# A new DMA model and offline priorities in a kernel's list scheduler, with re-laid DMA transfers: one adaLN transformer block on one Trainium2 core

## The chip, the cores and the metric

One NeuronCore of a Trainium2 chip. The metric is the device time of one launch in microseconds; lower is better. Ratios are the mean time of one kernel's fast runs over the mean of the other's fast runs of the same rounds, so they are not quite the ratios of the medians that are quoted. Profiles are of one execution each and are a microsecond or two shorter than the times, because they run from the first to the last instruction.

## The reference, cut to what matters

```python
mod = (silu(c) @ w_mod)                      # c: 1 x 640, w_mod: 640 x 3840 -> six vectors of 640
sa, ca, ga, sb, cb, gb = ...
h = layernorm(x) * (1 + ca) + sa             # x: 2048 x 640, bf16
qkv = h @ wqkv                               # 640 -> 3*640, 32 heads of 20
scores = q @ k.T * 20**-0.5                  # causal, window of 256 rows back
o = softmax(scores) @ v
x = x + ga * (o @ wo)
h = layernorm(x) * (1 + cb) + sb
x = x + gb * ((sigmoid(h @ w_gate) * (h @ w_up)) @ w_down)    # 640 -> 1536 -> 640
```

## The kernel before

All work is stated as operations with the tiles they read and write. A list scheduler inside the kernel's Python, run when the program is built, picks an order for each engine: it keeps a model of when each engine is free and how long each operation takes, and takes the ready operation with the lowest priority number. On the chip every engine then runs its list strictly in order. TensorE's list mixes small-tile attention matmuls with projections and MLP as filler. Nearly all DMAs are issued from SyncE's list.

A head has 20 columns, and four heads share one tile of 128 partitions, each at a multiple of 32. Projected Q and K come out of TensorE with other rows together, so they are written to a scratch in DRAM and read back in the arrangement for attention:

```python
def proj_qk(cc, mts, halves, prio):                  # chunk cc of 512 rows of x
    for which, (w, Rw) in enumerate(((wq, R_wq), (wk, R_wk))):
        ...                                          # scratch of this chunk: dram [640, 512]
        for mt in mts:
            ...                                      # 128 columns of Q or K for 512 rows: matmuls, eviction to s
            dma(d[mt * 128:(mt + 1) * 128, :], s.ap[:])
        for hh in halves:
            ...
            for j in range(4):                       # 20 partitions each, rows of 1 KB
                dma(t.ap[32*j:32*j + 20, :, :],
                    d.rearrange("(g r) c -> r g c", r=80)[j*20:(j+1)*20, 4*hh:4*hh + 4, :])
```

```python
if o.isdma:                                          # in the scheduler: one pipe of 330 GB/s
    s0 = max(st + dur + 0.3, bw)
    move = o.nbytes / 330e3
    bw = s0 + move
    o.end = s0 + move + o.fix
...
p_stg = sbpool("stg", 3, [128, 512])                 # staging buffers between projection and scratch
```

The first chunk's Q and K are projected "directly" instead: 640 small-tile matmuls that put each head at its partitions, no scratch. LayerNorm outputs of the later chunks are transposed by DMA. (In the listing of proj_qk the lambdas and the reads= and writes= lists are left out.)

The softmax here doesn't subtract the row's maximum and nothing guards it: scores larger than these inputs give would overflow.

## Time and profile before

| | before |
|---|---|
| time, median | 361.6 us (361.2 to 367.8 in 4 runs; the 367.8 counts as slow and is left out of the ratio) |
| profiled span | 358.6 us, granted clock 0.995 (another run, of 360.3 us) |
| TensorE busy | 339.7 us (95%) |
| TensorE idle | 18.9 us |
| DMA, main queue | 41% of 16 engines |

The lines behind this are shown in the prediction below. How they are read: the matmuls are pipelined and their ends are modelled in the profile, so 95% busy is not 95% of TensorE's peak; what TensorE waits for is in the list of waits; the DMA share of a window is the mean over the core's 16 DMA engines.

### The profile page before, as it was taken

The page shows a single profiled execution, that of the slowest core. Times are in us where ns is not written, and L with a number is a line of the kernel's source. Part 1 is how long each engine was busy: PE and PEld are TensorE (multiplying, and loading weights), DVE is VectorE, ACT ScalarE, POOL GpSimd, SP SyncE. Part 2 cuts the span into 40 slices and gives each one's busy share as a digit, 9 for nine tenths or more (in the row PEclk, how much of TensorE's full clock was granted, in tenths as well). Part 3 has the DMA queues.
Part 4 walks back from the last instruction along what each step waited for, and adds up shares of the span by engine and source line. Part 5 has one row for each costly group of instructions (what it writes and reads, how often), then busy time and mean ns, then how long its engine had stood idle before and what let it go on. Part 6 is the DMA issues. An engine that isn't in the chain of part 4 may idle for free.

```text
span 358.6 us, 10125 instructions
## 1 busy us (share of the span) xinstructions
PE 339.7 (95%) x4014; PEld 198.3 (55%) x4038; DVE 233.9 (65%) x504; ACT 223.6 (62%) x231; POOL 182.4 (51%) x304
## 2 busy tenths in 40 slices
PE   7989989989699999999999999999999999999996
PEld 3657556445235564445666534544664454788884
DVE  4569987994678977649787464776677755433342
ACT  1577876768648888887888788678678312022130
POOL 4227855985468975666676565566656201000000
PEclk9999999999989999999999999999999999999999
DMA  6988489696962652431281123003323010310101
GB/s 204 354 295 274 106 185 385 159 194 126 265 208 66 166 80 64 122 118 53 62 140 38 57 74 92 5 20 65 87 89 85 25 42 1 74 38 0 38 1 39
DMA packets 52672, 40.32 MB, mean 112 GB/s; under 512 B 22544, under 2 KB 49424, under 8 KB 52624
## 3 DMA queue, kind: packets, MB, share of 16 engines
q1 hardware_dynamic: 52624, 39.67, 40.7%
q8 instruction: 32, 0.52, 0.6%
q14 instruction: 16, 0.13, 0.1%
HBM read 25.89 MB, written 9.18 MB: 98 GB/s over the span
## 4 chain that ended last, share of the span: by engine, by line
PE 71%; DMA 9%; DVE 7%; SPq 4%; ACT 3%; issue 3%; POOL 1%; DVEq 0%; POOLq 0%
PE M L521 57%; PE S L522 7%; PE O L522 6%; SPq L438 4%; ACT E L802 3%; DMA oT<-doc 2%; DMA dq<-stg 2%; DMA x<-in_A_x_dram 2%; DVE x L602 2%; DMA hT<-x 1%; DMA big<-in_w_mod_dram 1%; PE M L522 1%; PE S L510 1%; DVE T L870 1%; DVE h2T L613 1%
## 5 line engine op out<-in xcount | busy, mean ns | idle before, releaser
L802 ACT ACTIVATE E<-S 128x2048 bf16<-128x2048 f32 (+1 forms) x104 | 171.3, 1647 | 43.2 <-PE S L522 40.4
L818 POOL TENSOR_SCALAR_AFFINE_SELECT E<-E 128x512 bf16<-128x512 bf16 x128 | 82.9, 657 | 84.7 <-ACT E L802 81.5
L521 PE MATMUL M<-h2T,wgu 128*128 128x256 bf16 (+1 forms) x708 | 110.8, 307 | 1.3 <-issue 0.8
L521 PEld LDWEIGHTS M<-h2T,wgu 128*128 128x128 bf16 x720 | 67.1, 98 | 35.5 <-issue 5.7
L820 POOL TENSOR_SCALAR_AFFINE_SELECT E<-E 128x512 bf16<-128x512 bf16 x112 | 73.6, 664 | 0.0
L928 ACT ACTIVATE sig<-M 128x256 f32<-128x256 f32 (+1 forms) x72 | 31.9, 454 | 56.7 <-PE M L521 56.6
L930 DVE SCALAR_TENSOR_TENSOR big<-sig,M 128x256 bf16<-128x256 f32 (+1 forms) x72 | 36.5, 507 | 44.8 <-PE M L521 36.2
L521 PE MATMUL M<-wd,big 128*128 128x320 bf16 x384 | 56.4, 299 | 0.0
L521 PEld LDWEIGHTS M<-wd,big 128*128 128x128 bf16 x384 | 36.5, 98 | 16.5 <-issue 1.9
L522 PE MATMUL S<-QT,KT 20*128 20x256 bf16 (+2 forms) x832 | 38.6, 259 | 3.0 <-ACT E L802 1.9
L522 PE MATMUL O<-E,V 128*32 128x256 bf16 (+2 forms) x832 | 32.4, 263 | 0.7 <-POOL E L818 0.7
L522 PEld LDWEIGHTS S<-QT,KT 20*128 20x128 bf16 x832 | 12.6, 92 | 34.6 <-ACT E L802 20.0
L940 DVE TENSOR_TENSOR x<-M,x 128x320 bf16<-128x320 f32 x32 | 15.6, 488 | 21.4 <-PE M L521 21.2
L870 DVE STREAM_TRANSPOSE T<-O 128x512 f32<-128x512 f32 x32 | 22.7, 711 | 9.6 <-PE O L522 9.0
L591 DVE BATCH_NORM_STATS2 st<-x 128x6 f32<-128x320 bf16 x64 | 27.1, 472 | 1.9 <-DMA x<-in_A_x_dram 1.7
L521 PE MATMUL M<-wo,oT 128*128 128x320 bf16 x160 | 26.1, 300 | 1.2 <-DMA oT<-doc 1.2
L521 PE MATMUL M<-wv,hT 128*128 128x320 bf16 x160 | 25.6, 300 | 1.0 <-DVE hT L651 1.0
L522 PEld LDWEIGHTS O<-E,V 128*32 128x32 bf16 x832 | 15.4, 95 | 15.9 <-issue 7.8
L521 PE MATMUL M<-hT,wk 128*128 128x512 bf16 x70 | 19.2, 398 | 4.1 <-DMA dq<-stg 3.8
L879 DVE STREAM_TRANSPOSE On<-Tn 128x512 bf16<-128x512 bf16 x32 | 22.5, 704 | 0.4
L667 DVE CAST stg<-M 128x512 bf16<-128x512 f32 x19 | 13.1, 690 | 14.3 <-PE M L521 14.2
L602 DVE TENSOR_SCALAR x<-x,st 128x640 bf16<-128x640 bf16 x32 | 19.9, 649 | 2.4 <-POOL st L599 2.3
(59 smaller groups left out, 280.3 us busy)
## 6 DMA issues: line engine op xcount, KB each, us to landing
x<-in_A_x_dram SPq DMA_DIRECT2D x32, 160.0 KB
big<-in_w_mod_dram SPq DMA_DIRECT2D x15, 320.0 KB
doc<-On SPq DMA_DIRECT2D x64, 40.0 KB
out_dram<-x SPq DMA_DIRECT2D x16, 160.0 KB
wgu<-in_B_w_gate_dram SPq DMA_DIRECT2D x5, 384.0 KB
wgu<-in_B_w_up_dram SPq DMA_DIRECT2D x5, 384.0 KB
wd<-in_B_w_down_dram SPq DMA_DIRECT2D x6, 320.0 KB
dq<-stg SPq DMA_DIRECT2D x15, 128.0 KB
```

What stands on the lines that cost most here:

```text
L521: return e.matmul(o, l, r, start=st, stop=sp, skip_group_check=True)
L522: return e.matmul(o, l, r, start=st, stop=sp, tile_position=tp, skip_group_check=True)
L591: ins = e.bn_stats(v(bi * 12 + j * 6, 6), src[bi].ap[:, j * 320:(j + 1) * 320])
L602: A("dve", lambda e, g, bi=bi: e.tensor_scalar(dst[bi].ap[:], src[bi].ap[:], v(48 + 2 * bi, 1), v(60 + bi, 1), op0=ALU.subtract, op1=ALU.m ...
L802: A("act", lambda e, eng, E=E, Sp=Sp, ncol=ncol: e.activation(E.ap[:, :, 0:ncol], Sp.ap[:, :, 0:ncol], ACT.Exp, scale=SM_SCALE), c_act(4 * ...
L818: return e.affine_select(ap, ap, pattern=[[0, 4], [1, 128]], compare_op=ALU.is_ge, fill=0.0, base=0, channel_multiplier=-1)
L820: return e.affine_select(ap, ap, pattern=[[0, 4], [-1, 128]], compare_op=ALU.is_ge, fill=0.0, base=-1, channel_multiplier=1)
L870: A("dve", lambda e, g: e.transpose(T1.ap[:], O.ap[:]), c_dve(512), reads=[O.r()], writes=[T1.r()], prio=4, tag="tr1")
L879: A("dve", lambda e, g: e.transpose(On.ap[:, half * 512:half * 512 + 512], Tn.ap[:]), c_dve(512), reads=[Tn.r()], writes=[On.r(half)], pri ...
L928: A("act", lambda e, g, pg=pg, sg=sg: e.activation(sg.ap[:, 0:W], pg.ap[:, 0:W], ACT.Tanh, scale=0.5), c_act(W), reads=[pg.r()], writes=[s ...
L930: A("dve", lambda e, g, pu=pu, sg=sg, ft=ft: e.scalar_tensor_tensor(out=hv(ft), in0=sg.ap[:, 0:W], scalar=1.0, in1=pu.ap[:, 0:W], op0=ALU. ...
L940: A("dve", lambda e, g, ps=ps, bi=bi, half=half: e.tensor_tensor(x1[bi].ap[:, half * 320:half * 320 + 320], ps.ap[:, 0:320], x1[bi].ap[:, ...
```

## The change

Intent: make the scheduler's picture of DMA truer (issue, descriptor rate, time for each descriptor, write receipt), choose the priorities offline so that the order stands up to random DMA delays, take work off the DMA queue, and read the Q/K scratch in rows of 4 KB. The core of the diff:

```diff
+                acc = max(st + 0.1, dge)
+                free[e] = max(st + dur, acc + 0.3)
+                dge = acc + 0.0018 * o.nd                        # nd: number of descriptors
+                bw = max(acc + 1.15, bw) + o.nd / 16e3 * (9 + o.nbytes / o.nd / 27.2)
+                o.end = bw + (1.2 if o.wr else 1.85)
...
+        o.prio = prio + PRIO.get(o.grp, 0.0)
+PRIO = {"x0": -9.5, "x1": -20.25, "wm0": 78.5, ... }             # 68 entries, cut
...
-    p_stg = sbpool("stg", 3, [128, 512])
+    p_stg = sbpool("stg", 6, [128, 512])
...                                     # c: one row of 1280 bytes and 5 tiny matmuls, not 640 runs of 2 bytes
...                                     # ln1: chunks 1 and 2 transposed on TensorE, evicted with scale and shift
...                                     # one scratch for Q and one for K, [92, 8, 512], used by all chunks
-                    dma(d[mt * 128:(mt + 1) * 128, :], s.ap[:])
+                dma(bass.AP(d.tensor, d.offset + mt * 4096, [[512, 8], [NDT * 4096, 16], [1, cw]]), s.ap[:, 0:cw])
...
-                for j in range(4):     # 4 DMAs of 20 partitions
+                if cw == 512:          # 1 DMA of 128 partitions, 12 rows in 32 not needed
+                    dma(t.ap[:], bass.AP(d.tensor, d.offset + 2048 * hh,
+                                         [[DH * 4096, 4], [4096, 32], [1, 2048]]), ..., nd=128)
...
-            proj_qk_direct(1, 13.6)    # second half of the first chunk
+            proj_qk(0, 12.7, 256, 256)
...                                     # attention pieces of two head groups packed into one tile of 2048
...                                     # attention output: 16 writes of 256 KB instead of 64 of 40 KB
```

(In the code cuts here and below the lambdas and the reads= and writes= lists are left out as well.)

## The prediction

> **What bounds the kernel now.** I read the page's first table, then the busy digits, then the groups by line with the shapes kept apart, then the table of ten-microsecond windows, the waits of TensorE alone, the chain of waits, and last the timeline of the stretches that stood out. Page and windows first:
>
> ```profile
> PE 339.7 (95%) x4014; PEld 198.3 (55%) x4038; DVE 233.9 (65%) x504; ACT 223.6 (62%) x231; POOL 182.4 (51%) x304
> PE   7989989989699999999999999999999999999996
> ...
> 0.00:10.00 10.00, 7.40 (x53) 3.58 (x54) 3.61 (x10) 1.49 (x2) 4.30 (x33) 1.00 0.69 219
> 20.00:30.00 10.00, 8.83 (x204) 6.27 (x206) 7.51 (x19) 6.70 (x9) 3.10 (x6) 1.00 0.81 277
> 90.00:100.00 10.00, 6.58 (x52) 3.03 (x54) 5.30 (x14) 5.33 (x5) 5.22 (x8) 0.99 0.96 279
> 300.00:310.00 10.00, 9.95 (x66) 6.29 (x65) 4.29 (x10) 1.20 (x2) 0.00 (x0) 1.00 0.31 51
> ```
>
> TensorE is busy for 339.7 of 358.6 us; the next engine stands at 65%. So the kernel is bound by TensorE, and idle TensorE time is only 18.9 us: about 2.6 in the first window, 3.4 in the window from 90 us, some 3 after the last matmul, the rest in crumbs. An upper limit follows at once: better waiting alone can give back perhaps 10 us. But busy is not full. I summed columns from the groups (count x columns / 2.4 GHz, divided by four where four small tiles run at once, which is an assumption of the sum): about 300 us for the whole program, 4 of them warm-up. By windows the sum fills some 0.75 of the time from 10 to 60 us, 0.58 from 90 to 100, about 0.84 from 100 to 280, and about 1.0 from 280 on. The timeline shows why it differs so:
>
> ```profile
> 222.54 0.29 PE L522 MATMUL S<-QT,KT 20*128 20x128 bf16 x8
> 222.77 0.51 PE L522 MATMUL O<-E,V 128*32 128x256 bf16 x16
> 223.21 1.25 PE L521 MATMUL M<-h2T,wgu 128*128 128x512 bf16 x5
> ...
> 339.79 9.44 PE L521 MATMUL M<-h2T,wgu 128*128 128x256 bf16 x85
> ```
>
> The score group holds TensorE for 0.23 us (to the next start) where its columns need 0.11; the attention-times-V group holds it 0.44 where they need 0.21. Against that, 85 matmuls of the last MLP take 111 ns each where columns need 107. So each small-tile group costs 0.1 to 0.2 us beyond its columns, at its change of form; such groups interleaved with MLP and projections are what makes 0.84 of 1.0. The waits of TensorE are short:
>
> ```profile
> PE M L521 <- DMA dq<-stg: 3.8, 2, 3.2
> PE S L522 <- ACT E L802: 1.9, 7, 0.5
> PE M L521 <- DMA oT<-doc: 1.2, 2, 0.8
> PE M L521 <- DVE hT L651: 1.0, 1, 1.0
> PE S L522 <- DMA KT<-dk: 0.9, 1, 0.9
> ```
>
> The largest is a projection that can't start because the three staging buffers are still being written to the scratch (3.2 us in one piece). From 300.3 to 355.8 us the chain of waits is one piece of TensorE work, the last MLP chunk, and the change doesn't touch it.
>
> **What the Trainium skill says.** "TensorE: Matmul & The Clock Gate", back-to-back issue gap: N/2.4 plus about 2.5 ns. The 111 ns for N = 256 agree (109). "TensorEngine Tiling (Array Packing)", key properties: "Mode switching requires drain". The 0.1 to 0.2 us above the columns agree with a drain per change of form, though the trace doesn't separate drain from weight loads. "DMA: Bandwidth & Descriptors", rules for kernel authors: one descriptor per contiguous run, so a strided last dimension gives one per element. The old load of the conditioning vector is 640 runs of 2 bytes; on the trace it is issued at 0.79 us, its reader starts at 3.77, and TensorE sees the first weight piece only at 6.15. The same page, "Why a DMA increments its semaphore by 16 and not by 1": the number of engines is the largest up to 16 that divides the slowest dimension of both sides. The old Q/K reads have 20 partitions, so 10 engines; the new big read has a DRAM side of 4 x 32 x 2048, so perhaps only 4. The trace of before doesn't show engines per transfer; this matters for a rival below.
>
> **The change, part by part.**
>
> 1. Second half of the first Q/K chunk. Removed: 320 small-tile matmuls of 256 columns (half of the two groups of 320) in 16 groups of 20. Start to start such a group takes 0.55 us (22.38 to 22.93 in the timeline), together 8.8 us. Added: 50 full matmuls of 256 columns at 111 ns, 5.6 us. Gain 3.2 us, all on TensorE. The result now goes through DRAM, some 5 us later, and is not needed at once.
>
> 2. Transposes of LayerNorm chunks 1 and 2. Removed: 8 of the 28 DMA transposes (issue 1.2 us each in the SyncE queue) and 10 scale-and-shift instructions of VectorE. Added: 40 TensorE transposes of 128 columns in 10 groups of four, and 10 evictions of 0.6 to 0.7 us on ScalarE or VectorE. The old group of such transposes has 20 in 2.5 us, 125 ns each, in isolated pairs; in fours I take 75 ns, an estimate between that and the 53 ns of the columns. Cost 3.0 us of TensorE. Gain: the chain's 4.2 us piece at 83.4 us ("DMA hT<-x") goes; but TensorE had other work then, so this is counted under 5.
>
> 3. Attention pieces packed over two head groups. For the three later chunks of two blocks, 8 rounds of 2048 columns and 8 of 1024 become 12 of 2048. So 104 exponentials, score groups and V groups become 92. ScalarE: 8 x (1.88 + 1.02) = 23.2 against 12 x 1.88 = 22.5 us a chunk, little. TensorE: the columns stay, 24 changes of form go; at 0.12 us each some 3 us.
>
> 4. Staging buffers from 3 to 6, one scratch, 4 KB rows. The read calls fall from 48 to 12 plus 16 small ones, the attention output from 64 writes to 16. The 3.8 us wait should go, also part of the SyncE queue's own issue time on the chain (3.9% of it). Gain 3.8 us.
>
> 5. Other exposed waits on DMA and on the engines fed by it (oT 1.2, KT 0.9, hT about 1.5): I take back 1.5 us in all.
>
> 6. Start. One descriptor instead of 640, x blocks 2 and 3 loaded before the modulation weights. First true projections now start at 12.9 us and there is a hole of 1 us at 21.6, waiting for the second half of hT. Gain 1.5 us; 0.3 MB more ahead of the weights costs about 0.9 of what the vector load gives back (at the 363 GB/s of the second window).
>
> 7. Order. New priorities and a delay model with issue and descriptor terms. This can't be counted from instructions. If the stretch from 10 to 60 us rises from 0.75 to 0.80 of its columns, it gives about 3 us; I take 3.
>
> Sum: -3.2 + 3.0 - 3.0 - 3.8 - 1.5 - 1.5 - 3.0 = -13.0. From 361.85 that makes 348.9; I say 348.5.
>
> **The rivals.** First, **work conservation**: TensorE is 95% busy, the last 75 us are solid, so earlier transfers only let it idle elsewhere. Parts 4 to 7 would then give only the 3.8 us, and 1 to 3 sum to -3.2: about 355, just outside or inside of 2%. For it: the waits are already short. Against it: the fill of 0.75 at the start and the hole at 95 to 99 us. Second, **the new Q/K read becomes the wait**: if it runs on 4 engines, each carries 128 KB; at 363 GB/s over 16 engines, 22.7 GB/s for one, that is 5.8 us a read, and the read brings 512 KB where 320 KB were needed. There is now one scratch for all chunks, so the next chunk's writes wait for these reads. That could hang 2 to 5 us on a projection in each of three chunks, and leave 355 to 360. Against it: projections are placed a chunk ahead, and the DMA is 41% busy on the main queue. Third, **the evictions**: transposes take three shared PSUM buffers for about 1 us each, ten times, and delay other chains; ScalarE and VectorE are near 0.8 to 0.9 in the windows from 30 to 130 us. A cost of 1 to 3 us: about 351. Fourth, **the order is worth much more** than I took: if the stretches up to 130 us reached the 0.84 of the later ones throughout, 8 us instead of 3, and the time is near 343.
>
> **Range and chances.** Even with everything good, the start (12 us), the end (3 us) and about 300 us of columns with 0.3 us a round for 92 rounds make some 340. Everything bad leaves about 359. I put 8 in 10 on 340.5 to 356.5. Faster by over 2% means under 354.6: the middle estimate lies 6 us below it, and it takes the first two rivals to cross it. Faster 0.82, within 2% 0.16, slower 0.02, as nothing added is on TensorE in an amount like that.
>
> **What would show it.** In the changed profile: 92 exponentials; the small-tile projections at 320 instead of 640; 60 transposes against the identity with under 6 us busy; no wait of TensorE for a scratch write over 0.5 us; the window from 90 to 100 us above 9 us busy; idle TensorE near 12 us in all instead of 18.9; the first projection before 12.5 us; the last 55 us unchanged. TensorE busy time should fall to about 334 us. The prediction is wrong if TensorE waits for Q or K reads by over 2 us, if idle time only moved elsewhere, or if busy time falls by less than 3 us.

## The result, and the profile after

The changed kernel takes 395.1 us in the median (394.8 to 399.0 in 4 runs) against 361.6: ratio 1.096, 95% interval 1.087 to 1.104. It is clearly slower where 348.5 was predicted, and outside the range.

The page of the changed kernel, first and second part:

```profile
PE 345.4 (88%) x3787; PEld 204.1 (52%) x3813; DVE 231.4 (59%) x500; ACT 225.7 (57%) x223; POOL 177.1 (45%) x300
PE   6899998196999953999399869999999999999996
PEclk9999999686999995899679969999999999999999
```

TensorE is busy 5.7 us longer, though some of its work went away, and idle for 48.0 us (393.4 - 345.4) instead of 18.9. The digits show five holes, of 3.0 to 10.7 us, and late in each hole and after it the granted clock is at half (by the clock records of the trace in five stretches of 6.8 to 13.7 us, 47.8 us together). The last quarter is as solid as before. So the time was lost in a few holes, not everywhere. What TensorE waited for, longest first:

```profile
PE M L539 <- DMA oT<-doc: 16.0, 2, 9.5
PE O L540 <- DVE T L941: 11.2, 2, 10.7
PE M L539 <- DVE V L717: 6.0, 2, 5.4
PE S L540 <- DMA KT<-dk: 3.0, 1, 3.0
```

These lines answer to the list of waits of before, whose longest was 3.8 us for the staging buffers. That one is gone. The new ones are waits for the attention output coming back (oT), for evictions by VectorE, and, least of the four, for the Q/K read itself.

One hole step by step. SyncE's queue and the engines after it, from the timeline (start, duration, engine and operation, idle time before it and its releaser):

```profile
128.60 1.23 SPq L461 DMA_DIRECT2D QT<-dq  x2
129.88 0.52 SPq L461 DMA_DIRECT2D KT<-dk  x1
...
133.74 11.75 SPq L640 DMA_TRANSPOSE h2T<-x  x2
...
149.99 0.35 DVE L645 TENSOR_SCALAR h2T<-h2T,scB,shB 128x256 bf16<-128x256 bf16 x1 [10.33 <-DMA h2T<-x]
152.76 0.70 DVE L941 STREAM_TRANSPOSE T<-O 128x512 f32<-128x512 f32 x1
153.61 0.62 PE L540 MATMUL O<-E,V 128*32 128x384 bf16 x8 [10.66 <-DVE T L941]
```

Three big Q/K reads are issued within 2 us. Two DMA transposes that follow take 11.75 us to issue; elsewhere in this profile one takes 1.2 us. VectorE stands for 10.3 us at the instruction that reads the transposes, which is next in its list; behind it in its list is the eviction of the attention output; and TensorE can't write the next attention output before that. The windows, with granted clock, DMA share and GB/s as the last three columns:

```profile
137.00:147.00 10.00, 5.95 (x46) 2.55 (x44) 1.79 (x3) 5.29 (x5) 3.62 (x6) 0.96 0.25 100
147.00:150.00 3.00, 0.00 (x0) 0.00 (x0) 0.01 (x1) 0.00 (x0) 0.00 (x0) 0.50 0.79 181
218.00:225.00 7.00, 6.73 (x77) 3.90 (x69) 1.86 (x4) 5.19 (x4) 3.98 (x7) 1.00 0.25 99
```

For ten and for seven microseconds on end the DMA share is 0.25, at 100 GB/s. A quarter is 4 engines in 16. Three reads of 512 KB at 100 GB/s take 15.7 us; from 130 us that makes 146, and the share rises again at about 147. By the same rate twelve such reads make some 63 us in which four engines are taken (an estimate).

The kept trace says more than the views. It has the time of every semaphore increment by which a DMA tells that data has landed. Each of the twelve big reads has one increment about 1 us after its issue and then four close together; a load of 128 partitions has 16. So the read lands in four parts. (A DMA whose outer dimension is 20 has ten late increments, and each of the new scratch writes, with an outer 8, has eight where the old ones had 16: these writes run on half of the engines, and do so in e1 below as well.) The three reads of the hole have all landed at 137.3, 143.1 and 148.1 us.

The increments also show what the reads do to other transfers. In the first of the five holes, the four oT reads are issued from 66.6 to 67.9 us. Twelve of the 16 increments of each have come by 68.6 to 70.5 us; the last four come at 75.2 to 77.2 us, together with the end of a big read (75.0 to 76.1 us), and TensorE goes on at 77.6. In the hole shown here it is not like that: all 16 increments of the two h2T transposes come together, at 149.1 to 149.2 and at 149.7 to 149.9 us, after the third read. There the whole transfer was late, not four parts of it.

### The profile page after: what moved, and what is told of

Same layout as the page of the kernel before. It is cut to its first block, busy times and chain, and to the rows that moved or that the text cites. A ratio compares the mean times of both kernels' runs of the same rounds, so it can differ in the third digit from the quotient of the medians.

```text
span 393.4 us, 9583 instructions
## 1 busy us (share of the span) xinstructions
PE 345.4 (88%) x3787; PEld 204.1 (52%) x3813; DVE 231.4 (59%) x500; ACT 225.7 (57%) x223; POOL 177.1 (45%) x300
## 5 line engine op out<-in xcount | busy, mean ns | idle before, releaser
L880 ACT ACTIVATE E<-S 128x2048 bf16<-128x2048 f32 (+1 forms) x92 | 169.2, 1840 | 63.1 <-PE S L540 57.5
L891 POOL TENSOR_SCALAR_AFFINE_SELECT E<-E 128x512 bf16<-128x512 bf16 x128 | 84.9, 666 | 64.9 <-ACT E L880 61.9
L893 POOL TENSOR_SCALAR_AFFINE_SELECT E<-E 128x512 bf16<-128x512 bf16 x112 | 74.3, 669 | 53.0 <-ACT E L880 41.4
L539 PEld LDWEIGHTS M<-h2T,wgu 128*128 128x128 bf16 x720 | 67.4, 98 | 35.8 <-issue 5.7
L539 PE MATMUL M<-wd,big 128*128 128x320 bf16 x384 | 58.3, 307 | 5.4 <-DVE V L717 5.4
L998 DVE SCALAR_TENSOR_TENSOR big<-sig,M 128x256 bf16<-128x256 f32 (+1 forms) x72 | 36.6, 508 | 43.1 <-PE M L539 33.5
L539 PE MATMUL M<-wo,oT 128*128 128x320 bf16 x160 | 29.1, 329 | 16.0 <-DMA oT<-doc 16.0
L540 PE MATMUL O<-E,V 128*32 128x256 bf16 (+2 forms) x832 | 31.7, 266 | 11.2 <-DVE T L941 11.2
L540 PE MATMUL S<-QT,KT 20*128 20x256 bf16 (+2 forms) x832 | 37.4, 265 | 3.6 <-DMA KT<-dk 3.0
L969 DVE TENSOR_TENSOR x<-M,x 128x320 bf16<-128x320 f32 x32 | 15.5, 483 | 26.3 <-PE M L539 26.0
L1008 DVE TENSOR_TENSOR x<-M,x 128x320 bf16<-128x320 f32 x32 | 15.7, 489 | 23.8 <-PE M L539 23.6
L539 PEld LDWEIGHTS M<-wo,oT 128*128 128x128 bf16 x160 | 15.4, 106 | 26.9 <-issue 18.4
L540 PEld LDWEIGHTS S<-QT,KT 20*128 20x128 bf16 x832 | 12.5, 93 | 31.9 <-ACT E L880 15.8
L941 DVE STREAM_TRANSPOSE T<-O 128x512 f32<-128x512 f32 x32 | 22.7, 709 | 10.7 <-PE O L540 10.4
L539 PE MATMUL M<-hT,wk 128*128 128x512 bf16 (+1 forms) x95 | 24.4, 407 | 0.8 <-issue 0.7
L539 PE MATMUL M<-wv,hT 128*128 128x320 bf16 x160 | 24.5, 300 | 0.6 <-DVE V L717 0.6
```

Of the source, the lines that this page charges most:

```text
L539: return e.matmul(o, l, r, start=st, stop=sp, skip_group_check=True)
L540: return e.matmul(o, l, r, start=st, stop=sp, tile_position=tp, skip_group_check=True)
L880: A("act", lambda e, eng, E=E, Sp=Sp, ncol=ncol: e.activation(E.ap[:, :, 0:ncol], Sp.ap[:, :, 0:ncol], ACT.Exp, scale=SM_SCALE), c_act(4 * ...
L891: return e.affine_select(ap, ap, pattern=[[0, 4], [1, 128]], compare_op=ALU.is_ge, fill=0.0, base=0, channel_multiplier=-1)
L893: return e.affine_select(ap, ap, pattern=[[0, 4], [-1, 128]], compare_op=ALU.is_ge, fill=0.0, base=-1, channel_multiplier=1)
L941: A("dve", lambda e, g: e.transpose(T1.ap[:], O.ap[:]), 0.71, reads=[O.r()], writes=[T1.r()], prio=4, tag="tr1")
```

## The experiments

The theory (A): the outer dimension of 4 in the source of the new read puts it on 4 of the 16 DMA engines. Each read takes 5.2 us there (512 KB at 100 GB/s), and every transfer issued meanwhile lands only when those four have served it too. Rivals: (B) the new order, made by the offline priorities, is fragile; (C) the extra bytes (512 KB read where 320 KB are needed). Four kernels were run at a time beside the kernel before on the same chip. All gave correct results.

**e1_split4: the read on 16 engines.** One read becomes four, one for each block of 32 partitions. Same bytes, same 4 KB rows; the order on TensorE, VectorE, ScalarE and GpSimd was compared and is the same as in the change.

```diff
-  dma(t.ap[:], bass.AP(d.tensor, d.offset + 2048 * hh, [[DH * 4096, 4], [4096, 32], [1, 2048]]))
+  for j in range(4):    # one operation to the scheduler, 4 DMAs on one semaphore
+      e.dma_start(t.ap[32*j:32*j + 32, :, :],
+                  bass.AP(d.tensor, d.offset + DH * 4096 * j + 2048 * hh, [[4096, 32], [1, 2048]]))
```

> The changed kernel with each of the twelve 512 KB Q/K reads issued as four DMAs of 32 partitions; same bytes, same 4 KB rows, same order of instructions on every engine but SyncE, which issues 36 more. Theory A (the read's source has an outer dimension of 4, so it runs on 4 of the 16 DMA engines and everything queued behind it on those waits): the stretches of 0.25 DMA share vanish, the five holes of TensorE (8 to 11 us each) go, and the time is 345 to 355 us. Rival B (the new priorities or the single scratch make the order fragile whatever the engines do): 385 to 400 us, holes stay. Rival C (the extra bytes, 512 KB read where 320 KB are needed): also unchanged within 2%, since the bytes are the same.

Measured: 348.7 us median (347.5 to 352.1), ratio to before 0.966 (0.957 to 0.975). 46 us faster than the change, and faster than before. Its page, its waits of TensorE and two windows (the second is the stretch in which the same three reads are issued):

```profile
PE 335.9 (97%) x3813; PEld 201.2 (58%) x3813; DVE 230.2 (66%) x500; ACT 225.7 (65%) x223; POOL 177.1 (51%) x300
PE   6899999899999989998999999999999999999996
```

```profile
PE M L539 <- ACT E L880: 1.1, 1, 1.1
PE O L540 <- DVE T L941: 1.0, 2, 0.5
PE M L539 <- DMA big<-in_w_mod_dram: 1.0, 3, 0.4
PE M L539 <- DMA oT<-doc: 0.8, 1, 0.8
```

```profile
90.00:100.00 10.00, 9.82 (x109) 4.90 (x108) 8.93 (x21) 8.01 (x7) 6.73 (x12) 1.00 0.74 239
111.00:122.00 11.00, 11.00 (x129) 7.10 (x127) 9.10 (x22) 9.95 (x11) 7.47 (x13) 1.00 0.73 188
```

The holes are gone, the stretch of 0.25 is 0.73, the clock stays at 1. Idle time of TensorE is 11.4 us, against 48.0. The difference of the two spans, 46.1 us, is 36.6 us less idle time and 9.5 us less busy time; the busy part fits the half clock after the holes, in which TensorE of the change was busy for 26.5 us. The three reads, from the first issue to the last landing, take 10.7 us here (111.4 to 122.0) and 19.5 in the change (128.6 to 148.1). Rivals B and C fall as causes of the loss by themselves: order and bytes are the same in both kernels.

**e2_colsplit_k4: the control for the split.** Also four DMAs of 128 KB for a read, but cut by columns, so each keeps the outer 4.

```diff
+  for g in range(4):
+      e.dma_start(t.ap[:, g, :], bass.AP(d.tensor, d.offset + 2048 * hh + 512 * g,
+                                         [[DH * 4096, 4], [4096, 32], [1, 512]]))
```

> The control for the split: again four DMAs of 128 KB per read and the same order, but cut by columns, so each keeps the outer dimension of 4 (128 rows of 1 KB). Theory A: still 0.25 DMA share, 390 to 405 us, about as slow as the change. If instead it was the size of one DMA, or the number of issues, that helped in the first run, this one is as fast as that: 345 to 355 us.

Measured: 395.5 us (393.4 to 397.1), ratio 1.093 (1.086 to 1.101). Two windows of its profile, with the DMA share as the last column but one:

```profile
138.00:146.00 8.00, 7.23 (x65) 3.23 (x57) 3.03 (x6) 6.57 (x5) 4.12 (x7) 1.00 0.28 92
219.00:224.00 5.00, 5.00 (x61) 2.94 (x59) 3.46 (x7) 4.20 (x6) 3.26 (x6) 1.00 0.26 77
```

As slow as the change. The size of a DMA or the number of issues is not what helped; the outer dimension is. (Its rows are 1 KB and not 4 KB, which this run does not hold fixed.)

**e3_pairs_k2: the dose.** Two DMAs for a read, each over two blocks, so the outer dimension is 2.

```diff
+  for j in range(2):
+      e.dma_start(t.ap[64*j:64*j + 64, :, :], bass.AP(d.tensor, d.offset + 2*DH*4096*j + 2048*hh,
+                                                      [[DH * 4096, 2], [4096, 32], [1, 2048]]))
```

> The dose: each read as two DMAs of 64 partitions, source with an outer dimension of 2. Theory A: 2 engines carry all, a DMA share of 0.125 in the stretches where only these reads run, some 10 us for one read instead of 5, and the time above 420 us. If the number of engines does not matter: near the time of the change or of the first run.

Measured, one run, state unknown: 451.1 us. Windows of its profile in which the DMA moves hardly anything else:

```profile
150.00:160.00 10.00, 10.00 (x97) 6.04 (x94) 7.11 (x16) 8.41 (x9) 7.03 (x13) 1.00 0.13 52
173.00:180.00 7.00, 0.00 (x0) 0.00 (x0) 0.00 (x0) 0.00 (x0) 0.00 (x0) 0.50 0.13 52
```

A share of 0.13 and half the rate: 2 engines of 16, and two late increments for each DMA. Outer dimension 32, 4, 2 makes 349, 395, 451 us, the last from a single run.

**e4_noprio: the change as it is, without the offline priorities.**

```diff
-        o.prio = prio + PRIO.get(o.grp, 0.0)
+        o.prio = prio + 0.0 * PRIO.get(o.grp, 0.0)
```

> The change as it is (reads on 4 engines) with the offline priorities set to zero, so the order is the list scheduler's own with the new delay model. Theory A: the read is slow whatever the order; still slower than before, 375 to 400 us. Rival B (the priorities are what makes it fragile): near 355 us.

Measured: 402.4 us (398.0 to 403.4), ratio 1.111. Slow with another order as well, so again not rival B.

**e5_split4_noprio: the same with the read repaired.**

> The repaired change (each Q/K read in four DMAs on 16 engines) with the offline priorities set to zero. Tells what the priorities are worth once the reads are mended. My prediction gave 3 us to the order as a whole: 351 to 354 us. If the priorities were chosen on a model that now holds, up to 10 us: 355 to 359. If they are worth nothing, 347 to 350.

Measured: 362.2 us (361.9 to 364.5), ratio 1.000 (0.993 to 1.007). Without the priorities the repaired change is as fast as before, within 0.7%. Against e1 they are worth 13.5 us by the medians, which are of different rounds and chips, and about 12 by the two ratios to before: more than I allowed in any branch. The scheduler's own estimate of the span, which it works out while it builds the program (so it stands in no profile; scheduling the kernels again gives it), is telling beside it:

| kernel | scheduler's own estimate | measured median |
|---|---|---|
| before (its old DMA model) | 348.8 | 361.6 |
| change | 344.9 | 395.1 |
| e1, repaired | 344.9 | 348.7 |
| e5, repaired, no priorities | 349.4 | 362.2 |
| e6, repaired, no packing | 350.6 | 357.0 |
| e7, repaired, chunk 1 by DMA | 453.0 | 469.9 |
| e8, change, ScalarE's queue | 389.0 | 436.8 |

Between e1 and e5 the estimate differs by 4.5 us and the chip by 13.5: the order chosen against random delays loses 4 us to what the model doesn't hold, the other 13. That fits the intent; two kernels don't prove it. And the change has the same estimate as e1: the model spreads every transfer over 16 engines (`o.nd / 16e3`), so it could not see the slow read.

**e6_split4_nopack: pieces packed within one head group.**

```diff
-            if a == 0:
+            if True:
                 sets = [x for g in gs for x in pieces_of(i0, QB, [g])]
```

> The repaired change with the attention pieces packed within one head group again, 104 exponentials instead of 92, priorities kept (but the order on every engine shifts somewhat, as the scheduler runs anew). My prediction: 24 more changes of form at 0.12 us, 3 us slower than the repaired change, 350 to 354 us. Rival: TensorE fills these rounds anyway, nothing over 1 us.

Measured: 357.0 us (356.0 to 358.6), ratio to before 0.984. It is 8.4 us slower than e1 by the medians of different rounds, about 7 by the ratios. But 5.7 of these are in the scheduler's own estimate, as the priorities were chosen for the other set of operations; the run bounds the packing, it doesn't isolate it.

**e7_split4_pet2: chunk 1 transposed by DMA again** (`PET = (2,)`).

> The repaired change with LayerNorm chunk 1 transposed by DMA again, chunk 2 on TensorE; order shifts. My prediction: TensorE saves 5 groups of four transposes (1.5 us of busy time), and waits of VectorE and TensorE for hT come back: 347 to 353 us in all. If the DMA transposes were the important part: 355 or more.

Measured: 469.9 us (469.2 to 471.1). A miss that says nothing of transposes: the estimate itself was 453, so the scheduler, with priorities made for other operations, built a bad order. In its profile TensorE runs at half clock from 260 to 340 us, busy for 1.2 to 5.0 us of every ten.

**e8_actqueue_k4: the slow reads issued from ScalarE's queue**, scheduled anew.

> The change as it is, reads on 4 engines, but issued from ScalarE's queue instead of SyncE's; order shifts. If what hurts is that everything issued later by SyncE stands behind the reads in the same queue (theory A as I state it), the holes shrink: DMA transposes issue in 1 to 3 us each instead of up to 12 for two, and the time is 355 to 375 us. If it is only the bandwidth of those 4 engines, or ScalarE is now blocked by its own waits, the holes stay: 385 to 405 us.

Measured: 436.8 us, one run. Again confounded: its estimate was 389. The DMA transposes were quick to issue here (18 of 20 in 1.2 to 1.7 us, two in 2.0 and 2.1), as expected, and the time was no better. The next pair does it properly.

**e9_actq_sameorder and e10_actq_split4: queue order or engines?** The order is made as in the change, then the twelve reads move to ScalarE's list at their place in time; once on 4 engines (e9), once in four DMAs on 16 (e10).

```diff
     P.schedule()
+    big = [o for o in P.order["sp"] if o.isdma and o.tag == "qkr" and o.nbytes == 524288]
+    P.order["sp"] = [o for o in P.order["sp"] if o not in big]
+    for o in big:
+        o.eng = "act"
+    P.order["act"] = sorted(P.order["act"] + big, key=lambda o: o.start)
```

> The earlier run with the reads in ScalarE's queue was confounded: the list scheduler made another order of it and itself counted 389 us for it. Here the order is made as in the change and only then are the twelve reads moved, at their place in time, from SyncE's stream to ScalarE's; TensorE, VectorE and GpSimd keep their order. Reads still on 4 engines. If later transfers suffer because they stand behind the reads in one queue, the holes shrink: no DMA transpose issue above 4 us, 355 to 375 us. If the 4 engines' bandwidth is what counts whatever the queue, 385 to 405 us.

> The control to the run before it: the same move to ScalarE's queue, with each read in four DMAs on 16 engines. Tells what the move itself costs (ScalarE waits at the issue for the scratch writes): 348 to 358 us. The difference between the two is the price of 4 engines when nothing else stands behind them in the queue; to be set against the 46 us between the change and the repaired change.

Measured: e9 395.6 us (391.9 to 396.0 in its three fast runs, one run slow), ratio 1.088; e10 360.4 us (358.3 to 362.0), ratio 0.996. So 4 engines still cost 35 us with none of SyncE's transfers standing behind the reads in one queue. In the change they cost 46. The move itself is not free: e10 is 11.7 us slower than e1 (about 11 by the ratios). Up to some 11 us may thus belong to the shared queue; this pair doesn't say. TensorE waits for the same things as in the change. From SyncE's timeline and the waits of TensorE in e9:

```profile
135.89 3.27 SPq L640 DMA_TRANSPOSE h2T<-x  x2
213.68 18.01 SPq L640 DMA_TRANSPOSE h2T<-x  x4
```

```profile
PE M L539 <- DMA oT<-doc: 14.4, 2, 8.2
PE M L539 <- DVE V L717: 12.0, 2, 7.1
PE O L540 <- DVE T L941: 9.4, 2, 8.9
```

The first two transposes are issued in 3.27 us instead of 11.75, and land hardly earlier: at 147.3 to 149.1 and 150.3 to 150.5 us. (The 18.01 us of the second line include a pause of 9.1 us between issues; the longest single issue is 4.25 us.)

I had stated theory A as "everything issued later stands behind the reads in the same queue". As the whole explanation that falls. What holds is the four engines: a transfer spread over 16 engines has a share on each of the four taken ones, and it lands with its last share. In e9 this is so across queues: of a load that SyncE issues at 130.6 us, twelve increments come by 134.3 us and the last four at 137.3 to 138.1. I counted in the kept traces the transfers with 16 increments whose last four came over 2 us after the other twelve:

| before | change | e1 | e2 | e4 | e9 | e10 |
|---|---|---|---|---|---|---|
| 0 of 151 | 14 of 148 | 0 of 148 | 14 of 148 | 25 of 148 | 8 of 148 | 0 of 148 |

Of these kernels they occur in the ones with the slow read and in no other. Why the DMA transposes are late as a whole, in either queue, is not shown.

**e11_before_stg6: six staging buffers in the kernel before**, nothing else.

> The kernel before with six staging buffers instead of three and nothing else (its list scheduler makes a somewhat different order; by its own count 350.8 us instead of 348.8). My prediction gave 3.8 us to the buffers: 357 to 359 us if the wait just goes; 360 to 363 if TensorE's wait only moves or the order eats it.

Measured: 366.4 us (363.8 to 367.1), ratio 1.010 (1.004 to 1.016). The buffers alone don't help, though the run doesn't hold the order fixed: the order that comes with them is a little worse (2.0 us by the scheduler's estimate).

**e12_split4_noprio_direct: step 1 taken back, on the base of e5.**

```diff
-            proj_qk(0, 12.7, 256, 256)
+            proj_qk_direct(1, 13.6)
```

> The repaired change without priorities (362.2 us), with the second half of the first Q/K chunk projected by small tiles directly again. My prediction's step 1: 3.2 us of TensorE work more, so 364 to 367 us; the scheduler's own count says 354.6 against 349.4, so up to 5 us. If the staged way gains nothing, 360 to 363.

Measured: 365.5 us (364.2 to 366.7), 3.3 us above e5 (its own estimate 5.2 above).

## Why the prediction was wrong

**The step that failed is the second rival: its path, and with it its size.** I had the cause: the page of the Trainium skill "DMA: Bandwidth & Descriptors", "Why a DMA increments its semaphore by 16 and not by 1", on how many engines a transfer gets, the pattern 4 x 32 x 2048, "so perhaps only 4", and 5.8 us a read. The runs show 5.2 us and 4 engines. What failed is who would wait: "2 to 5 us on a projection in each of three chunks", 355 to 360 at the worst. I asked who reads the result of the slow transfer, and found slack. The wait for the read itself is indeed only 3.0 us. I did not ask who else needs those four engines. The waits came to the attention output (16.0 us), and through VectorE's list, where instructions that wait for the transposes stood ahead of evictions (11.2 and 6.0 us). Repairing the read gave 46 us back (e1). I also took the mean DMA load of 41% for slack, where a mean over 16 engines says nothing of four. And I left out that each of these holes costs twice, as the clock is at half after it: with this go the 9.5 us of busy time in the 46.

**"Slower 0.02"** rested on "nothing added is on TensorE in an amount like that". That bounds the added work of TensorE, not the added waiting. "Everything bad leaves about 359" has no sum behind it: 2 to 5 us in each of three chunks on 348.5 already makes 354.5 to 363.5, not 355 to 360. At the other end, the parts of "some 340" add up to 342.6 as written.

**The sum of parts, set beside e1,** comes out at -13.0 us as predicted (361.7 to 348.7), but by luck: steps 1, 2, 3 and 7 as measured already add up to -17.1, and not all of that is time of the kernel. Step by step:

- Step 1, predicted -3.2: e12 against e5 gives -3.3. Right, as far as two orders can be compared.
- Step 2, predicted +3.0: 60 transposes in e1 take 5.8 us of busy time, 20 took 2.5 before. Right: +3.3 of busy time.
- Step 3, predicted -3.0: score and V groups of TensorE fall from 71.0 to 67.4 us of busy time on the pages. Right: -3.6 of busy time.
- Step 4, predicted -3.8: the wait of 3.8 us is 0.4 in e1, but the buffers alone make the kernel before no faster (e11). Right as to the wait, not shown as to the time.
- Step 5, predicted -1.5: TensorE's waits for oT and KT fall from 2.1 to 0.8 us. Right in direction, not isolated.
- Step 6, predicted -1.5 with the first projection before 12.5 us: it starts at 13.7 in e1, where it was 12.9. Wrong at the start; the hole at 21.6 us did go (the window from 20 to 30 us is busy 10.00 instead of 8.83).
- Step 7, predicted -3.0 for the order: 13.5 us. Badly mis-sized. Without the priorities e5 equals before, so the other steps together gave nothing under the scheduler's plain order, although most can be seen in busy time or waits. That is what the first rival, work conservation, said; that it is the reason isn't shown.

Of the signs named for the profile, e1 shows 335.9 us of busy time (about 334 predicted), 11.4 us idle (near 12), 92 exponentials and 9.82 us busy in the window from 90 to 100. The change as it was shows all the signs named for being wrong: a wait of 3.0 us for the Q/K read, more idle time (48.0 us), and busy time that rose by 5.7 us.

**What stays open:** why the transposes land late as a whole, how much of the 46 us is the shared queue, how the 13.5 us of the priorities come about, and what the packing is worth alone. Any edit of the set of operations makes the scheduler build another order, and that can move the time by more than the edit (e7).

## What to carry to other kernels

Look at the outer dimension of both sides of every DMA pattern; where it is small and can't be merged with the next, cut the transfer along it so that each part has a multiple of 16 outside. A slow transfer with slack of its own can still stall others that share its engines, and an engine that works through its list in order hands the delay on; so read the DMA share of a stretch as a number of engines out of 16, not only as a mean. And before a list scheduler's variant is put on a chip, compare the scheduler's own estimate, or the run measures the order and not the edit.

## What the Trainium skill lacked or had wrong

- "DMA: Bandwidth & Descriptors", why a DMA increments its semaphore by 16: the rule for the number of engines is right here (share 0.25 for an outer 4, 0.13 for 2). It lacks what this does to other transfers: an oT read had twelve of its 16 increments 2 us after its issue and the last four 7 us later, and the kernel took 395.1 us instead of 348.7, with only 3.0 us of waiting for the slow read itself.
- The same page, rules for kernel authors, says of two transfers to disjoint partition halves "Don't bother" and asks for one 128-partition transfer. Here one transfer of 128 partitions cut into four of 32 made the kernel 46 us faster (395.1 to 348.7), because the one had an outer 4 on the DRAM side. The row's reason, that both halves go over all 16 engines, didn't hold here. Another row of the same table, "Use all 16 engines", has the condition; the two rows are not tied together.
- The same page gives no time for issuing a DMA transpose of one 128 x 640 tile within SBUF on Trainium2; what it has for earlier chips is for other shapes. Here one takes 1.2 us of SyncE's list as a rule, and two took 11.75 us while four engines were busy with earlier reads.
- "TensorE: Matmul & The Clock Gate", PE-mode transpose, gives about 275 ns for a 128 x 128 transpose in a kernel. Here one ordinary matmul against an identity lasts 221 ns in the mean, but they overlap: 60 of them, in twos and fours, took 5.8 us of busy time, so about 97 ns each, and the 40 added ones, in fours, about 83 (5.8 - 2.5 over 40). No page has a time for transposes done in this way.
